# Windowed attention into a SwiGLU block: the opening's value products grouped by row mode, pair 3 on a joined tile, and two gate blocks at once

## The chip, the cores and the metric

The kernel runs on one core of a Trainium2 chip. The metric is the time of one execution on the device in microseconds (us), the median of several runs. A profile is one more execution, taken by the hardware profiler.

## What is computed

```python
def _attn_ref(q, k, v):                     # q, k, v: (8 batches, 8 heads, 576, 64)
    scores = scale * np.matmul(q, k.transpose(0, 1, 3, 2))
    mask = (rel >= 0) & (rel < 64)          # rel = row position - column position
    scores = np.where(mask, scores, -1e9)
    ...                                     # softmax over the columns
    return np.matmul(attn, v)

def _moe_ref(x, w_gate, w_val, w_out):      # x: 4608 tokens x 512, of the attention's output
    g = x @ w_gate                          # 512 x 1536
    silu = g * (1.0 / (1.0 + np.exp(-g)))
    val = x @ w_val
    return silu * val @ w_out               # 1536 x 512
```

Every token looks at itself and the 63 tokens before it, in each of 8 heads; the heads' outputs side by side are a token's 512 inputs to a gated two-layer block.

## The kernel before

The 4608 tokens are worked off in nine tiles of 512: eight hold rows 0 to 511 of a batch, one (`LAST`) the rows 512 to 575 of all eight. For each tile the kernel makes scores, exponentials, sums and value products, then the gate and value products with `wg` and `wv` in twelve blocks of 128 columns (`gate_value`, L432 to L440: four products of 128x512 with `wg` and four with `wv` to a block), then the projection with `wo` (L445). From the second tile on, the attention of a tile lies among the projection of the one before, so that TensorE always has work.

The order is written out by hand; each engine executes its own instructions in the order in which they stand in the program, and waits only where an operand or a buffer is not ready. Eight PSUM banks are used under the names `bank[0]` to `bank[7]`: banks 0 to 3 are the halves of two double tiles, `two0` and `two1`, banks 4 to 7 are `one0` to `one3`. In the profile all of them show as `two` and `one`.

The change touches the opening, tile 0, for which nothing can be prepared. Its heads are handled as four pairs `u` = 0 to 3. `scores_first(u)` (L233) writes a pair's scores into `two0` or `two1`, `weigh_first(u)` (L563) takes their exponential on ScalarE (ACT) into `eb[u]`, `sums_first(u, b)` (L568) sums them over the rows with a product with ones (L295) and gives two functions that make the inverse of the sums on ACT, a logarithm (L316) and an exponential (L319).

`part_first(us, x, ms)` (L345) issues the value products of tile 0. A pair's output has eight blocks `m` of 64 tokens. An odd block needs the 64 keys of its own block and the 64 before it, which lie in the same tile of 128 value rows `v1[:, m // 2]`: one product over 128 rows for each head `h`. An even block's keys lie in two neighbouring tiles, in rows 64 to 127 of the one before (`x` = 1) and in rows 0 to 63 of its own (`x` = 0): two products over 64 rows each, block 0 only one. A pair thus has 22 products. Pairs 0 to 3 accumulate in banks `aos = (4, 5, 0, 1)`.

Products over the upper and the lower 64 rows of the array may run at the same time, and both kinds add to the same bank. `marker` (L358) is a small product over all rows that stands between them; `look` (L361) issues a marker and lets VectorE (DVE) copy one column of it into `seen`.

The four tiles of values come by different ways: `v1[:, 0]` is cast by ACT (L624), `v1[:, 1]` by DVE (L630), both from float32 that SyncE's queue loaded; tiles 2 and 3 come straight into place by two transfers that GpSimd (POOL) issues at 6.6 and 7.7 us. Behind these two, POOL issues the weights in chunks, `wg` and `wv` in turn: for blocks 0 and 1 in two halves each, then 256 columns (two blocks) to a chunk, with a part of the next tile's keys `k_r` and queries `q_s` between them, then `wo` and the next tile's values `vb`.

`scale(t, u, o_ps)` (L382 on) multiplies a pair's output by the inverse sums on DVE and writes a quarter `c` = `u` of `xT` (L392). `gate_part(0, (0, 1), pairs, c)` (L412) issues the products of quarter `c` alone for blocks 0 and 1 with `wg` and `wv` (L416), four products, so that the gate stage can begin before all pairs are scaled. The order from the last scores on, before the change, is:

```python
    part_first((0, 1), 1, (2, 6, 4))
    part_first((2,), 1, (2, 6, 4))
    look(7)
    log2, inv2 = sums_first(2, 6)
    part_first((0, 1), 0, (1, 3, 5))
    marker(7)
    ...
    part_first((3,), 0, (1, 3, 5))
    log3, inv3 = sums_first(3, 7)
    ...
    gate_part(0, (0, 1), pairs, 1)
    part_first((3,), 0, (0, 2, 4, 6, 7))
    for c in (2, 3):
        scale(0, c, bank[aos[c]])
        gate_part(0, (0, 1), pairs, c)
```

Half of pair 3's products so stand between the gate parts 1 and 2. Then the twelve blocks follow: for blocks 0 and 1 only `gate_end` (the activation on ACT, L429, and the multiply on DVE, L430), for the others the whole `gate_value` (L436), one block after the other, in banks that alternate between 5 and 7 and 4 and 6. The `mask` for the later tiles is built on DVE after block 2 (L667 to L674). Transposes of `k_r` (L681) stand after blocks 7 and 10.

Of the kernel before, what the change touches and what calls it, by code (L numbers as in the profile page):

```python
# [8 lines left out]
P = 128  # L9
# [8 lines left out]
def kernel(  # L18
# [10 lines left out]
    nc = tc.nc  # L29
    S, D, H = 576, 64, 8  # L30
# [23 lines left out]
    v1 = v12[:, 0]  # L54
# [59 lines left out]
    def second_halves(t, us, a, copy):  # L114

        src, dst = slice(64 * a, 64 * a + 32), slice(64 * a + 32, 64 * a + 64)
        ap = staged[t][0][:, us].rearrange("r u (e d) -> r (u e) d", d=D)
        copy(ap[dst, :, 0:32], ap[src, :, 32:64])
# [78 lines left out]
    def split_k(dst, tp, copy=nc.vector.tensor_copy):  # L197
        copy(  # L198
            dst.rearrange("p (r e) -> p r e", e=4),
            tp.rearrange("p (e r) -> p r e", e=4),  # L200
        )
# [20 lines left out]
    def bias_first(u):  # L222

        for c in range(2):
            for h in range(2):
                r = slice(64 * h, 64 * h + 64)
                nc.tensor.matmul(
                    two[u % 2][64 * c:64 * c + 64, h], identb[r, r],
                    bias[r, c ^ h].rearrange("r e i c x -> r (e i c x)"),
                    start=True, stop=False,  # L230
                )

    def scores_first(u):  # L233

        qT = queries[0][:, u, :]
        for j in range(8):
            c = j % 2
            for h in range(2):
                r = slice(64 * h, 64 * h + 64)
                nc.tensor.matmul(  # L240
                    blocks(two[u % 2][64 * c:64 * c + 64, h], 0, j, min(8, j + 2)),
                    kT[0][r, u, 64 * j:64 * j + 64],
                    blocks(qT[r], 0, j, min(8, j + 2)),
                    start=False, stop=j > 5,
                )
# [3 lines left out]
    def half(x):  # L249
        return slice(64 * x, 64 * x + 64)  # L250
# [60 lines left out]
    def turned(ap):  # L311

        return ap.rearrange("r (e x) -> r x e", e=16)
# [28 lines left out]
        for w in range(2):  # L342
            invert(rs[w])

    def part_first(us, x, ms):  # L345

        for m in ms:
            for u in us:
                r = slice(0, P) if m % 2 else half(x)
                for h in range(2):  # L350
                    nc.tensor.matmul(  # L351
                        blocks(bank[aos[u]][half(h)], 0, m, m + 1),
                        v1[r, m // 2 if m % 2 or not x else m // 2 - 1, 2 * u + h, :],
                        blocks(weights[0, u][r, h, :], 0, m, m + 1),
                        start=(m, x) == (2, 1), stop=m == 7,
                    )

    def marker(b):  # L358
        nc.tensor.matmul(bank[b][0:D, 0:16], ones[:, 0:D], ones[:, 0:16])

    def look(b):  # L361
        marker(b)
        nc.vector.tensor_copy(seen[:], bank[b][0:D, 0:1])

    def mix(t, w, o):
        E = [weights.pop((t, w, h))[0] for h in range(2)]
# [18 lines left out]
    def scale(t, u, o_ps):  # L385
        if u == 0:
            xT[t] = att.tile([P, 4, 512], BF16, name="xT", tag="xT")
        x, r = xT[t][:, u, :], inverse.pop((t, u))
        if t == NT - 1:
            x, o_ps = x.rearrange("r (x e) -> r x e", e=16), turned(o_ps)  # L390
            r = r.rearrange("r (x e) -> r x e", e=16)
        nc.vector.tensor_mul(x, o_ps, r)  # L392
# [10 lines left out]
    def d_tile():  # L403
        return bank[6 + take("v")]

    def mix_all(t):
# [3 lines left out]
        for u in range(4):  # L410
            scale(t, u, tiles[u // 2][:, u % 2])

    def gate_part(t, ms, tiles, c):
        for i, w in enumerate((wg, wv)):
            for m, pair in zip(ms, tiles):
                nc.tensor.matmul(  # L416
                    pair[i], w[:, c, P * m:P * m + P], xT[t][:, c, :],
                    start=(c == 0), stop=(c == 3),
                )

    def gate_tiles():
        return out_tile(), d_tile()

    def gate_end(t, m, pair):
        if m == 0:
            hT[t] = hpool.tile([P, 12, 512], BF16, name="hT", tag="hT")
        g_ps, v_ps = pair
        sg = fsb.tile([P, 512], FP32, name="sg", tag="sg")
        nc.scalar.activation(sg[:], g_ps[:], AF.Silu)  # L429
        nc.vector.tensor_mul(hT[t][:, m, :], sg[:], v_ps[:])  # L430

    def gate_value(t, m):  # L432
        pair = gate_tiles()
        for ps, w in zip(pair, (wg, wv)):
            for c in range(4):
                nc.tensor.matmul(  # L436
                    ps[:], w[:, c, P * m:P * m + P], xT[t][:, c, :],
                    start=(c == 0), stop=(c == 3),
                )
        gate_end(t, m, pair)  # L440
# [32 lines left out]
    def out_tile():  # L473
        return bank[4 + take("g")]
# [33 lines left out]
    set_exp()  # L508
    nc.vector.memset(ones[:, 0:P], 1.0)
    nc.vector.memset(ones[:, P:512], 1.0)  # L510
    make_identity(nc, identb[:])
    warm = bank[7]

# [34 lines left out]
    on_v, on_p, on_a = nc.vector.tensor_copy, nc.gpsimd.tensor_copy, nc.scalar.copy  # L548
# [14 lines left out]
    def weigh_first(u):  # L563
        E = eb[u][:, 1:17].rearrange("r (h y) z -> r h (y z)", h=2)
        nc.scalar.activation(E, two[u % 2][:], AF.Exp, scale=0.125)
        weights[0, u] = E

    def sums_first(u, b):  # L568
        totals_first(u, bank[b])
        inverse[0, u] = room(1)[:, 0]  # L570
        return lambda: log(inverse[0, u], bank[b]), lambda: invert(inverse[0, u])
# [51 lines left out]
    log1()  # L623
    on_a(v1[:, 0], v_first[:, 0])  # L624
    weigh_first(2)
    bias_first(3)
    scores_first(3)
    weigh_first(3)
    inv1()
    on_v(v1[:, 1], v_first[:, 1])  # L630
    aos = (4, 5, 0, 1)
    part_first((0, 1), 1, (2, 6, 4))
    part_first((2,), 1, (2, 6, 4))
    look(7)
    log2, inv2 = sums_first(2, 6)
    part_first((0, 1), 0, (1, 3, 5))
    marker(7)
    part_first((0, 1), 0, (0, 2, 4, 6, 7))
    part_first((2,), 0, (1, 3, 5, 0, 2, 4, 6, 7))
    log2()  # L640
    inv2()
    part_first((3,), 1, (2, 6, 4))
    pairs = [(bank[4], bank[6]), (bank[2], bank[3])]
    scale(0, 0, bank[aos[0]])
    look(3)
    part_first((3,), 0, (1, 3, 5))
    log3, inv3 = sums_first(3, 7)
    log3()
    inv3()
    gate_part(0, (0, 1), pairs, 0)  # L650
    scale(0, 1, bank[aos[1]])
    gate_part(0, (0, 1), pairs, 1)
    part_first((3,), 0, (0, 2, 4, 6, 7))
    for c in (2, 3):
        scale(0, c, bank[aos[c]])
        gate_part(0, (0, 1), pairs, c)
    taken["g"] = taken["v"] = 1
    set_silu()
    for m in range(12):
        if m < 2:  # L660
            gate_end(0, m, pairs[m])
        else:
            gate_value(0, m)
        if m == 2:
            for x in range(2):
                for c in range(2):
                    nc.vector.tensor_copy(  # L667
                        mask[half(x), 0, c],
                        tri[half(x), x ^ c].rearrange("r (y e) -> r e y", e=16),
                    )  # L670
            for i in (1, 2, 4):
                nc.vector.tensor_copy(mask[:, i:2 * i], mask[:, 0:i])
            for E in eb:
                nc.vector.memset(E[:, 0], 0.0)  # L674
        if m in (7, 10):
            for i in range(2):
                u = m // 10 * 2 + i
                tp = two[i].bitcast(BF16)[:, 0, 0:512]
                for e in range(4):
                    for h in range(2):  # L680
                        nc.tensor.transpose(  # L681
                            tp[half(h), P * e:P * e + P], raw_k[:, 2 * u + h, e], identb[:]
                        )
                split_k(kT[1][:, u, :], tp, on_a if u == 2 else on_v)
        if m == 8:
            second_halves(1, lo, 1, on_v)
            second_halves(1, lo, 0, on_a)
        if m == 9:
            for u in range(2):
                turn_q(1, u)  # L690
# [98 lines left out]
```

## Time and profile before

| what | us |
|---|---|
| median of 3 runs | 326.29 |
| the runs | 326.08 to 326.31 |
| profiled execution, its own time | 325.92 |
| its span, first to last instruction | 324.2 |
| PE busy | 315.3 (97%) |
| DVE busy | 218.2 (67%) |
| ACT busy | 166.9 (51%) |
| POOL busy | 145.4 (45%) |

The profile names the engines PE (TensorE; its weight loads are PEld), DVE (VectorE), ACT (ScalarE), POOL (GpSimd) and SP (SyncE). A row of the timeline has the start in us, the length in us, the engine, the line, the operation, what it writes and reads, the shapes and how many instructions were merged; in brackets stands how long the engine had been idle and what ended that. Matmuls overlap in the array, so a single one's length is more than the distance to the next. A row of the chain of waits has the start, the length and the work, merged, with a count. The chain follows what released what, back from the end.

### The profile page before, as it was taken

How to read it: one execution, taken by the hardware profiler on the slowest of the kernel's cores; microseconds unless marked ns; L12 is line 12 of the kernel's file. 1: busy time of each engine (PE TensorE's matmuls, PEld its weight loads, DVE VectorE, ACT ScalarE, POOL GpSimd, SP SyncE). 2: the span in 40 equal slices, each digit the busy share in tenths (PEclk: the TensorE clock that was granted, in tenths of full speed). 3: DMA queues.
4: the chain of work that ended last, by engine and by line, in shares of the span. 5: the costliest groups of instructions: out<-in, count | busy, mean ns of one | idle time of the engine just before them, and what ended most of it. 6: DMA issues, size and time to landing. Idle time of an engine off the chain costs nothing.

```text
span 324.2 us, 7017 instructions
## 1 busy us (share of the span) xinstructions
PE 315.3 (97%) x2738; PEld 151.0 (47%) x2781; DVE 218.2 (67%) x347; ACT 166.9 (51%) x239; POOL 145.4 (45%) x259
## 2 busy tenths in 40 slices
PE   7989999999999999999999999999999999999996
PEld 3644445444544444444444444454444544444443
DVE  4665756498676776887678766876687586774422
ACT  5943666347633673358336743565347633773310
POOL 4955666875085794676224989463200000000000
PEclk9999999999999999999999999999999999999999
DMA  7999999999879999949922999699501400021013
GB/s 250 202 196 198 207 148 197 164 166 114 166 153 200 138 172 188 192 56 227 200 33 32 164 180 95 45 202 189 99 3 30 103 2 0 10 86 40 0 27 104
DMA packets 83521, 40.35 MB, mean 124 GB/s; under 512 B 64160, under 2 KB 78752, under 8 KB 83488
## 3 DMA queue, kind: packets, MB, share of 16 engines
q0 software_dynamic: 51488, 22.59, 58.5%
q1 hardware_dynamic: 31456, 16.79, 21.4%
q10 hardware_dynamic: 544, 0.52, 0.5%
q8 instruction: 21, 0.34, 0.5%
q14 instruction: 12, 0.10, 0.1%
HBM read 53.02 MB, written 9.44 MB: 193 GB/s over the span
## 4 chain that ended last, share of the span: by engine, by line
PE 95%; DMA 1%; issue 1%; DVE 1%; ACT 1%; DVEq 0%
PE one L436 56%; PE one L445 28%; PE two L269 3%; PE two L376 2%; PE one L302 1%; DMA q_f<-in_q_dram 1%; PE one L487 1%; PE one L416 1%; PE one L195 0%; PE two L416 0%; PE two L351 0%; DVE kT L198 0%; PE one L351 0%; PE two L240 0%; PE two L681 0%
## 5 line engine op out<-in xcount | busy, mean ns | idle before, releaser
L429 ACT ACTIVATE sg<-one 128x512 f32<-128x512 f32 x107 | 63.9, 597 | 115.0 <-PE one L436 87.2
L430 DVE TENSOR_TENSOR hT<-sg,one 128x512 bf16<-128x512 f32 x107 | 74.1, 693 | 61.7 <-PE one L436 59.5
L436 PE MATMUL one<-xT,wg 128*128 128x512 bf16 x414 | 108.0, 379 | 0.8
L436 PE MATMUL one<-xT,wv 128*128 128x512 bf16 x416 | 107.2, 379 | 0.2
L445 PE MATMUL one<-wo,hT 128*128 128x512 bf16 x396 | 93.5, 380 | 1.5 <-issue 0.3
L126 POOL DMA_DIRECT2D k_s<-in_k_dram x112 | 60.6, 550 | 25.2 <-DMA q_s<-in_q_dram 17.3
L436 PEld LDWEIGHTS <-wv 128*128 128x128 bf16 x424 | 41.5, 98 | 50.0
L436 PEld LDWEIGHTS <-wg 128*128 128x128 bf16 x424 | 41.3, 98 | 49.7
L445 PEld LDWEIGHTS <-hT 128*128 128x128 bf16 x420 | 39.0, 98 | 46.7 <-issue 2.0
L282 ACT ACTIVATE eb<-two 128x960 bf16<-128x960 f32 (+1 forms) x32 | 29.5, 974 | 15.1 <-PE two L269 15.0
L217 DVE STREAM_TRANSPOSE kT<-k_s 128x512 bf16<-128x512 bf16 x28 | 36.0, 1287 | 0.0
L285 DVE TENSOR_TENSOR eb<-eb,mask 128x960 bf16<-128x960 bf16 (+1 forms) x32 | 21.0, 658 | 11.9 <-ACT eb L282 11.9
L392 DVE TENSOR_TENSOR xT<-two,r 128x512 bf16<-128x512 f32 x34 | 21.7, 685 | 7.6 <-PE two L376 4.8
L177 POOL CAST vb<-v_f 128x512 bf16<-128x512 f32 x20 | 11.4, 617 | 34.3 <-PE one L436 11.7
L319 ACT ACTIVATE r<-r 128x512 f32<-128x512 f32 (+1 forms) x34 | 22.2, 655 | 1.0
L207 DVE STREAM_TRANSPOSE qT<-q_s 128x512 bf16<-128x512 bf16 x32 | 22.2, 700 | 0.1
L316 ACT ACTIVATE r<-one 128x512 f32<-128x512 f32 x31 | 18.3, 590 | 4.8 <-PE one L302 4.7
L91 POOL DMA_DIRECT2D q_s<-in_q_dram x24 | 13.0, 556 | 4.7 <-DVE qT L207 4.7
L290 DVE TENSOR_TENSOR both<-eb 128x512 bf16<-128x512 bf16 x32 | 13.6, 425 | 1.1
L152 POOL DMA_DIRECT2D vb<-in_v_dram x16 | 10.9, 687 | 6.0 <-DMA wo<-in_moe_w_out_dram 3.8
L495 ACT ACT_TABLE_LOAD x9 | 11.5, 1283 | 2.0 <-issue 1.9
L98 POOL DMA_DIRECT2D q_s<-in_q_dram x16 | 8.6, 629 | 7.1 <-DVE qT L207 7.1
(123 smaller groups left out, 192.2 us busy)
## 6 DMA issues: line engine op xcount, KB each, us to landing
k_s<-in_k_dram POOLq DMA_DIRECT2D x112, 56.0 KB, 4.8
q_s<-in_q_dram POOLq DMA_DIRECT2D x24, 248.0 KB, 5.6
v_f<-in_v_dram SPq DMA_DIRECT2D x40, 128.0 KB
wg<-in_moe_w_gate_dram POOLq DMA_DIRECT2D x5, 256.0 KB, 8.9
wv<-in_moe_w_val_dram POOLq DMA_DIRECT2D x5, 256.0 KB, 9.0
q_f<-in_q_dram SPq DMA_DIRECT2D x4, 256.0 KB
wo<-in_moe_w_out_dram POOLq DMA_DIRECT2D x2, 512.0 KB, 10.7
vb<-in_v_dram POOLq DMA_DIRECT2D x16, 64.0 KB, 4.1
```

The costliest lines, as they stand in the source:

```text
L126: nc.gpsimd.dma_start(k_s[p0:p0 + 32, g, :, 0:w], k[b, a:H:2, s:s + P].rearrange("u (r e) d -> r u (e d)", e=4) [:, :, 32 * c:32 * c + w],)
L207: nc.vector.transpose(queries[t][:, u, :].rearrange("r (e x) -> r e x", e=16), staged[t][0][:, u].rearrange("r (e d) -> r e d", d=D)[:, :, ...
L217: nc.vector.transpose(dst[:, u, :].rearrange("r (g x e) -> r g e x", g=4, e=4), k_s[:, :, u].rearrange("r g (e d) -> r g e d", d=D)[:, :, ...
L282: nc.scalar.activation(flat, s_ps[h][:].rearrange("r a b -> r (a b)")[:, 0:n], AF.Exp, scale=0.125)
L285: nc.vector.tensor_mul(flat, flat, mask[:].rearrange("r j c e y -> r (j c e y)")[:, 0:n])
L316: nc.scalar.activation(r, d_ps, AF.Ln)
L319: nc.scalar.activation(r, r, AF.Exp, scale=-1.0)
L392: nc.vector.tensor_mul(x, o_ps, r)
L429: nc.scalar.activation(sg[:], g_ps[:], AF.Silu)
L430: nc.vector.tensor_mul(hT[t][:, m, :], sg[:], v_ps[:])
L436: nc.tensor.matmul(ps[:], w[:, c, P * m:P * m + P], xT[t][:, c, :], start=(c == 0), stop=(c == 3),)
L445: nc.tensor.matmul(o_ps[:], hT[t][:, c, P * s:P * s + P], wo[:, c, :], start=(c == 0), stop=(c == 11),)
```

## The change

The value products of tile 0 are put in another order, with products of one row mode together. Those of pair 3 use a second copy of its values: in `joined`, which lies in the memory of `mask` until that is built, an even block's keys stand in one tile of 128 rows (the last 64 rows of the tile before in the upper half, with zeros there for block 0, and the first 64 rows of its own tile in the lower half), so that each even block is one product over 128 rows. DVE fills `joined` with two copies and a memset. All value products, pair 3's too, stand ahead of the gate parts, and four of pairs 0 and 1 ahead of the last scores. The marker is now a product over the 64 rows whose products stand beside it. After the gate parts, blocks 2 and 3 are issued together: all products with `wg` of both, then all with `wv` of both. The mask is built after block 3 instead of block 2.

```diff
-    def part_first(us, x, ms):
+    def part_first(us, x, ms, last=None):
...
-                        start=(m, x) == (2, 1), stop=m == 7,
+                        start=(m, x) == (2, 1), stop=m == last,
...
+    joined = mask[:].rearrange("r j c e y -> r (j c e y)")[:, 0:512]
+    joined = joined.rearrange("r (i h d) -> r i h d", i=4, h=2)
+
+    def joined_first(u):
+
+        for m in range(8):
+            for h in range(2):
+                src = v1[:, m // 2, 2 * u + h] if m % 2 else joined[:, m // 2, h]
+                nc.tensor.matmul(
+                    blocks(bank[aos[u]][half(h)], 0, m, m + 1),
+                    src, blocks(weights[0, u][:, h, :], 0, m, m + 1),
+                    start=m == 0, stop=m == 7,
+                )
+
+    def marker(b, x):
+        nc.tensor.matmul(bank[b][0:D, 0:16], ones[half(x), 0:D], ones[half(x), 0:16])
...
+    nc.vector.memset(joined[half(1), 0], 0.0)
...
+    aos = (4, 5, 0, 1)
     bias_first(3)
+    part_first((0, 1), 1, (2,))
     scores_first(3)
     weigh_first(3)
     inv1()
     on_v(v1[:, 1], v_first[:, 1])
-    aos = (4, 5, 0, 1)
-    part_first((0, 1), 1, (2, 6, 4))
+    on_v(joined[half(1), 1:4], v1[half(1), 0:3, 6:8])
+    part_first((0, 1), 0, (1, 5))
+    part_first((0, 1), 1, (6, 4))
     part_first((2,), 1, (2, 6, 4))
-    look(7)
+    marker(7, 1)
+    on_v(seen[:], bank[7][0:D, 0:1])
+    on_v(joined[half(0)], v1[half(0), :, 6:8])
+    part_first((0, 1), 0, (3,))
     log2, inv2 = sums_first(2, 6)
-    part_first((0, 1), 0, (1, 3, 5))
-    marker(7)
-    part_first((0, 1), 0, (0, 2, 4, 6, 7))
-    part_first((2,), 0, (1, 3, 5, 0, 2, 4, 6, 7))
+    part_first((0, 1), 0, (7,))
+    marker(7, 0)
+    for u in range(3):
+        part_first((u,), 0, (0, 2, 4, 6), 6 if u < 2 else None)
+    scale(0, 0, bank[aos[0]])
     log2()
     inv2()
-    part_first((3,), 1, (2, 6, 4))
-    pairs = [(bank[4], bank[6]), (bank[2], bank[3])]
-    scale(0, 0, bank[aos[0]])
-    look(3)
-    part_first((3,), 0, (1, 3, 5))
     log3, inv3 = sums_first(3, 7)
     log3()
     inv3()
-    gate_part(0, (0, 1), pairs, 0)
-    scale(0, 1, bank[aos[1]])
-    gate_part(0, (0, 1), pairs, 1)
-    part_first((3,), 0, (0, 2, 4, 6, 7))
-    for c in (2, 3):
-        scale(0, c, bank[aos[c]])
+    part_first((2,), 0, (1, 3, 5, 7), 7)
+    joined_first(3)
+    pairs = [(bank[4], bank[6]), (bank[2], bank[3])]
+    for c in range(4):
+        if c:
+            scale(0, c, bank[aos[c]])
         gate_part(0, (0, 1), pairs, c)
     taken["g"] = taken["v"] = 1
     set_silu()
     for m in range(12):
-        if m < 2:
+        if m < 4:
+            if m == 2:
+                pairs += [gate_tiles(), gate_tiles()]
+                for i, w in enumerate((wg, wv)):
+                    for n in (2, 3):
+                        for c in range(4):
+                            gate_one(0, n, pairs[n][i], w, c)
             gate_end(0, m, pairs[m])
         else:
             gate_value(0, m)
-        if m == 2:
+        if m == 3:
```

`gate_one` is the single product that `gate_part` issued before.

More of the change, by code (lines that the diff above doesn't have):

```diff
@@ L354, in part_first @@
                         blocks(weights[0, u][r, h, :], 0, m, m + 1),
-                        start=(m, x) == (2, 1), stop=m == 7,
+                        start=(m, x) == (2, 1), stop=m == last,
                     )
[L358 to L363, printed above, removed]
+    joined = mask[:].rearrange("r j c e y -> r (j c e y)")[:, 0:512]
[11 more added lines that the diff above has]
+        nc.tensor.matmul(bank[b][0:D, 0:16], ones[half(x), 0:D], ones[half(x), 0:16])
     def mix(t, w, o):
@@ L411, in mix_all, with gate_one @@
             scale(t, u, tiles[u // 2][:, u % 2])
+    def gate_one(t, m, ps, w, c):
+        nc.tensor.matmul(
+            ps, w[:, c, P * m:P * m + P], xT[t][:, c, :], start=(c == 0), stop=(c == 3)
+        )
     def gate_part(t, ms, tiles, c):
@@ L415, in gate_part @@
             for m, pair in zip(ms, tiles):
[L416 to L419, printed above, removed]
+                gate_one(t, m, pair[i], w, c)
     def gate_tiles():
```

## The prediction

> **What bounds the kernel now.** I read the page first, for the engine that fills the span, then the chain of waits of the first 60 us, then the timeline of the opening, and last the landing of single transfers.
>
> ```profile
> span 324.2 us, 7017 instructions
> PE 315.3 (97%) x2738; PEld 151.0 (47%) x2781; DVE 218.2 (67%) x347; ACT 166.9 (51%) x239; POOL 145.4 (45%) x259
> PE 95%; DMA 1%; issue 1%; DVE 1%; ACT 1%; DVEq 0%
> ```
>
> TensorE (PE) is the chain for 95% of the span. Once the gate products run without a hole, whatever moves their start moves the end by as much, as long as nothing that does not move with PE (a transfer) is late. So the question is: when does the first whole gate step (L436) begin, and does the rest follow?
>
> The chain of waits around the change (start, length, engine and line, count):
>
> ```profile
> 11.90 0.39 PE two L240 x14
> 12.29 0.18 PE one L351 x8
> 12.95 0.24 PE one L295 x2
> 13.19 0.19 PE one L351 x12
> 13.38 0.55 PE one L351 x20
> 13.94 0.70 PE two L351 x22
> 14.87 0.22 PE one L295 x2
> 15.09 0.32 PE one L416
> 16.93 0.41 PE two L351 x10
> 17.43 0.70 DVE xT L392
> 18.17 0.38 PE one L416
> 20.06 5.83 PE one L436 x27
> 36.27 0.57 PE two L681 x16
> 48.84 0.97 PE two L376 x64
> ```
>
> The value products (L351) of head pairs 0 to 3 run from 12.29; gate parts (L416) start; then ten value products of pair 3 at 16.93, and PE stands until DVE (VectorE) has scaled pair 2. The timeline of the same stretch shows the hole:
>
> ```profile
> 11.77 0.66 DVE L630 CAST v<-v_f 128x512 bf16<-128x512 f32 x1
> 13.81 0.59 ACT L316 ACTIVATE r<-one 128x512 f32<-128x512 f32 x1
> 14.02 0.69 DVE L392 TENSOR_TENSOR xT<-one,r 128x512 bf16<-128x512 f32 x1 [0.88 <-PE one L351]
> 14.43 0.63 ACT L319 ACTIVATE r<-r 128x512 f32<-128x512 f32 x1
> 15.02 0.39 PE L416 MATMUL one<-xT,wg 128*128 128x512 bf16 x1
> 17.43 1.29 DVE L392 TENSOR_TENSOR xT<-two,r 128x512 bf16<-128x512 f32 x2 [1.83 <-PE two L351]
> 18.17 0.38 PE L416 MATMUL one<-xT,wg 128*128 128x512 bf16 x1 [0.86 <-DVE xT L392]
> 19.90 1.03 PE L436 MATMUL one<-xT,wg 128*128 128x512 bf16 x4
> ```
>
> DVE itself was idle for 1.83 us before scaling pair 2. It waited for PE: pairs 2 and 3 share the buffer `two0`, and the wait that the scale gets ends with pair 3's last products, which stand behind half of the gate parts. The first whole gate step begins at 19.90.
>
> **Unit prices.** The chain's x12, x20 and x22 rows hold products of one size. Twelve in one row mode take 0.19, so 0.0158 each. The x20 row changes mode twice (64 rows, 128 rows): 0.55 - 20 x 0.0158 leaves 0.23, so 0.117 a change. The x22 row changes three times: 0.70 - 22 x 0.0158 = 0.35, again 0.117. A gate product costs 5.83 / 27 = 0.216; the 16 of the gate parts cost 3.45 with no hole. Before, they took 19.90 - 15.02 = 4.88, so 1.43 went into the hole and the ten products.
>
> **Part 1: products regrouped, pair 3 joined.** Before, from the end of the last scores (12.29) to the first gate product, PE does 78 value products (12 + 6, 12, 20, 22, 6), seven mode changes, three markers and two pairs of totals. After, pair 3 takes 16 full-row products instead of 22; four products of pairs 0 and 1 go ahead of the last scores; and all of pair 3 comes before the gates: 88 - 6 - 4 = 78 again. But there are five mode changes (to 128 rows for blocks 1 and 5, to 64, to 128 for blocks 3, 7 and the totals, to 64 for the even blocks, to 128 for the rest) and two markers.
> Sum: 78 x 0.0158 = 1.23, 5 x 0.117 = 0.59, totals 0.24 + 0.22, markers 0.03: 2.30. The chain's stretch was 15.09 - 12.29 = 2.80, so gates start 0.50 earlier, at 14.52. The difference is two changes (0.23), a marker, and the old wait of about 0.2 for the second value tile's cast (DVE, ends 12.43), which the blocks 1 and 5 now fill.
> The four early products need the first value tile's cast on ACT and lie in PE's old wait for the last key split (before 11.90): nothing, or, if the cast were late, that lateness on all that follows.
>
> **Part 2: new DVE work.** A zero fill of 64x128 lies in DVE's idle start: nothing. Two copies into the joined tile, 64x384 and 64x512, stand in DVE's queue behind the cast that ends at 12.43, and ahead of the first scale. Their nearest row, that of the POOL transfer that ran beside it, and the transfers of the last two value tiles, for the fourth of which the second copy waits:
>
> ```profile
> 23.46 0.88 DVE L672 COPY mask<-mask 128x128 bf16<-128x128 bf16 x3
> 23.51 0.75 POOL L181 DMA_DIRECT2D wv<-in_moe_w_val_dram  x1 [0.42 <-DMA wg<-in_moe_w_gate_dram]
> L144 POOL DMA_DIRECT2D v<-in_v_dram x2: 891/969/1047, 6.6 to 7.7; - x2
> DMA to landing us min/median/max: 5.2/5.4/5.5
> ```
>
> Those three copies (128, 256 and 512 columns) take 0.88 together, so the new ones, 896 columns as well, should take at most about that, and from below nothing. I take the upper end. The fourth tile lands at 7.7 + 5.2 = 12.9, before the second copy's turn. From 12.43, with the small `seen` copy and its marker between them, DVE is free by about 13.5. Pair 0's even blocks leave PE at 12.29 + 1.3 = 13.6 at the latest; the first scale starts then and ends near 14.3, ahead of 14.52. So the copies cost nothing on PE's path; without that cover they would cost up to 0.88.
>
> **Part 3: gate parts in one run.** Scale by scale: pair 0 ends by 14.3, pair 1 by 15.0 (needed at 15.4), pair 2 after its inverse (ACT, ends 15.06) at 15.8 (needed at 16.25). Pair 3's logarithm and inverse follow on ACT at 0.59 and 0.63, so about 16.3; scaled by 17.0, needed at 14.52 + 12 x 0.216 = 17.1. That is close: 0.1 of slack. No hole, so the whole step starts at 14.52 + 3.45 = 17.97 in place of 19.90: a gain of 1.93.
>
> **Part 4: two blocks at once, mask later.** Sixteen products either way: 0. The order (both gate, then both value) asks for the second chunk of `wv` four products (0.86) later. Block 3's gate products now come right behind block 2's, into block 0's bank, which block 0's activation must have left; it can start once the last gate part's first product is done, eight products (1.7) earlier, and takes about as long as the logarithm above, 0.59: nothing. The mask's build on DVE moves behind one more multiply. Before, block 3's multiply stood behind it and the 27 products from 20.06 ran without a hole; now block 4's does, in the same change of banks: nothing.
>
> **What is late next: transfers.** POOL (GpSimd) issues the weights in the same order as before. Each answer below is for one transfer alone (issue time, then us to landing):
>
> ```profile
> L181 POOL DMA_DIRECT2D wv<-in_moe_w_val_dram x1: 735/735/735, 10.7 to 10.7; - x1
> DMA to landing us min/median/max: 5.8/5.8/5.8
> L181 POOL DMA_DIRECT2D wg<-in_moe_w_gate_dram x1: 789/789/789, 11.4 to 11.4; - x1
> DMA to landing us min/median/max: 6.4/6.4/6.4
> L181 POOL DMA_DIRECT2D wv<-in_moe_w_val_dram x1: 806/806/806, 13.6 to 13.6; - x1
> DMA to landing us min/median/max: 8.4/8.4/8.4
> L77 POOL DMA_DIRECT2D k_r<-in_k_dram x1: 742/742/742, 24.8 to 24.8; - x1
> DMA to landing us min/median/max: 9.0/9.0/9.0
> L152 POOL DMA_DIRECT2D vb<-in_v_dram x1: 679/679/679, 43.2 to 43.2; - x1
> DMA to landing us min/median/max: 3.1/3.1/3.1
> ```
>
> Half a chunk of `wv` for gate parts 2 and 3 lands at 16.5, needed at 14.52 + 10 x 0.216 = 16.7. `wg` for blocks 2 and 3 lands at 17.8, needed at 17.97. `wv` for blocks 4 and 5 lands at 22.0, needed 20 products after 17.97, at 22.3. All fit, by 0.2 to 0.3; the last also caps the gain: the whole steps cannot start before 22.0 - 4.32 = 17.7, a gain of 2.2. Further on, the second half of `k_r` lands at 33.8 for transposes (L681) that move from 36.27 to 34.3, and the last of `vb` at 46.3 for products (L376) that move from 48.84 to 46.9. The rest of the chain then moves whole.
>
> **Sum.** 1.93 us off, of the profiled execution's own 325.92 (span 324.2 and 1.7 around it): 324.0. The median of the runs is 326.29, 0.37 above that execution; against it, rounded to 1.9: **324.4**. Lower bound of the gain if the opening saves nothing: 1.43; upper 2.2; so 324.1 to 324.9. Runs scatter by 0.23 (326.08 to 326.31), which widens this to 323.9 to 325.1. A difference of 0.2%, 0.65 us, is about what a measurement tells from none.
>
> **Rivals.**
> *Copies and issues hold each other up.* The two copies run in the time in which POOL issues a transfer every 0.8 us. If a copy had to wait for a running issue to end, the first would end near 13.2 and the second behind the 0.806 us issue of 13.6, at about 14.8; the first scale ends at 15.45, and whole steps start at 18.95: gain 0.95, 325.3. Against it, the three mask copies ran through a POOL issue begun 0.05 after them, in 0.88. For it, the issue there was the later one.
> [...]
> *The weights take the hole's place.* If the chunks land one issue (0.8) later, `wv` for block 4 comes at 22.8 and PE loses 0.5 of the gain: 324.9.
> *The gain is absorbed later*: `k_r` or `vb`, by rows 0.5 early, come 2 us late. 326.3, no change. Nothing on PE waits for a transfer in the chain after 20 us.
> *Slower.* The same weights, delayed for good: POOL sends each transfer once an earlier one is back, so lost issue time could add up. Only if `wv` for block 4 lands over 2.2 us late is the gain used up; at 3.0 late whole steps start at 25.0 - 4.32 = 20.7, 0.8 after the old start: 327.1. Against it: two copies of 0.88 in all cannot hold POOL that long, and transfers land 6 to 8 us after issue, with a queue to live on.
>
> **How the numbers follow.** Forecast 0.72; copies held up 0.08; weights late 0.06; absorbed 0.07; slower 0.07. The first three are faster: 0.86. The range reaches from 323.9 to the held-up copies, 325.3, and leaves out some 0.15.
>
> **What would show it.** Right: no idle PE over 0.2 us between 12.3 and the first whole gate step, which starts near 18.0; transposes of `k_r` near 34.4. Wrong: PE waits for `xT` on DVE (part 2 or 3 mis-sized), for a weight chunk, or the later stages start as late as before.

## The result

The changed kernel took 324.38 us (median of 7 runs, 324.13 to 324.97), the kernel before 326.29 us (7 runs, 325.87 to 327.97): a ratio of 0.9938, 95% interval 0.9919 to 0.9957. The profiled execution took 324.13 us, its span was 322.4.

The page of the changed kernel, with its instruction queue, which is wanted further on:

```profile
span 322.4 us, 7047 instructions
PE 317.1 (98%) x2774; PEld 150.5 (47%) x2774; DVE 219.5 (68%) x349; ACT 166.8 (52%) x239; POOL 145.8 (45%) x259
...
q8 instruction: 21, 0.34, 0.4%
...
PE 95%; DMA 2%; DVE 1%; SPq 1%; issue 0%; DVEq 0%
```

PE is the chain for 95% of the span, as before; the span is 1.8 shorter. Where that comes from is seen when both opening and later stages are cut at the same five events: the last scores, the first gate product, the first whole step, the second transposes of `k_r`, the mixing products with `vb`. A row has the window, its length, then each engine's busy time. The changed kernel first:

```profile
11.72:14.37 2.65, 2.65 (x100) 2.24 (x101) 2.38 (x6) 2.62 (x5) 2.65 (x5) 1.00 1.61 189
14.37:18.09 3.72, 3.62 (x22) 1.57 (x17) 1.82 (x3) 3.36 (x5) 3.06 (x5) 1.00 1.46 195
18.09:34.47 16.38, 16.38 (x91) 7.42 (x91) 11.47 (x26) 7.17 (x12) 8.77 (x14) 1.00 1.39 199
34.47:47.05 12.58, 12.58 (x138) 5.76 (x142) 7.91 (x15) 8.56 (x10) 8.29 (x13) 1.00 1.47 167
```

The kernel before:

```profile
11.90:15.02 3.12, 3.11 (x101) 2.43 (x101) 1.53 (x5) 3.09 (x5) 3.12 (x5) 1.00 1.56 191
15.02:19.90 4.88, 3.97 (x28) 1.88 (x28) 1.87 (x3) 3.00 (x5) 3.60 (x6) 1.00 1.46 199
19.90:36.27 16.37, 16.27 (x89) 7.42 (x91) 11.07 (x26) 7.16 (x12) 8.80 (x14) 1.00 1.36 198
36.27:48.84 12.57, 12.46 (x137) 5.75 (x142) 7.91 (x15) 8.55 (x10) 8.37 (x15) 1.00 1.46 170
```

The first stage shrank from 3.12 to 2.65, the second from 4.88 to 3.72, the third and fourth are as long as before (16.38 for 16.37, 12.58 for 12.57). So the change itself brought 0.47 + 1.16 = 1.63; another 0.18 of the 1.81 by which the whole steps start earlier lies in the last scores, which came at 11.72 instead of 11.90 in this execution. They waited for keys that DVE had still to copy (into `kT`, until 11.67 and 11.85; the scores started 0.05 later in both), not for the few changed products ahead of them, and in variants of the changed kernel that are alike up to there they came at 11.71 to 11.90; the 0.18 is put down to chance. What is won by 18.09 is kept whole.

The timeline of the changed opening:

```profile
11.40 0.25 PE L351 MATMUL one<-eb,v 64*64 64x64 bf16 x4
...
11.61 0.58 DVE L645 CAST v<-v_f 128x512 bf16<-128x512 f32 x1
...
12.28 0.35 DVE L646 COPY mask<-v 64x384 bf16<-64x384 bf16 x1
...
12.65 0.78 POOL L181 DMA_DIRECT2D wg<-in_moe_w_gate_dram  x1
...
12.96 0.58 DVE L652 COPY mask<-v 64x512 bf16<-64x512 bf16 x1
...
13.52 1.29 DVE L402 TENSOR_TENSOR xT<-one,r 128x512 bf16<-128x512 f32 x2
...
14.37 0.39 PE L424 MATMUL one<-xT,wg 128*128 128x512 bf16 x1
...
14.92 0.69 DVE L402 TENSOR_TENSOR xT<-two,r 128x512 bf16<-128x512 f32 x1
...
15.24 0.38 PE L424 MATMUL one<-xT,wg 128*128 128x512 bf16 x1
...
15.72 0.38 PE L424 MATMUL two<-xT,wg 128*128 128x512 bf16 x1
...
16.06 0.69 DVE L402 TENSOR_TENSOR xT<-two,r 128x512 bf16<-128x512 f32 x1 [0.45 <-ACT r L319]
...
17.23 0.38 PE L424 MATMUL one<-xT,wg 128*128 128x512 bf16 x1
...
18.09 1.89 PE L424 MATMUL one<-xT,wg 128*128 128x512 bf16 x8
```

The 0.86 hole is gone: the scale of pair 2 starts at 14.92, pair 3 is scaled by 16.75, and the fourth gate part follows at 17.23 without a wait. One stop that nothing forecast is left: the product of 15.24 should be followed 0.22 later, at 15.46, and the next starts at 15.72. That is 0.26 us, on no wait that the row names, so not every stop of an engine in these traces is a wait for an operand or a buffer that the record shows. That stop is what most of the later runs are about.

### The profile page after: what moved, and what is told of

Same layout as the page of the kernel before. It is cut to its first block, busy times and chain, and to the rows that moved or that the text cites. A ratio compares the mean times of both kernels' runs of the same rounds, so it can differ in the third digit from the quotient of the medians.

```text
span 322.4 us, 7047 instructions
## 1 busy us (share of the span) xinstructions
PE 317.1 (98%) x2774; PEld 150.5 (47%) x2774; DVE 219.5 (68%) x349; ACT 166.8 (52%) x239; POOL 145.8 (45%) x259
## 3 DMA queue, kind: packets, MB, share of 16 engines
q1 hardware_dynamic: 31456, 16.79, 21.0%
## 4 chain that ended last, share of the span: by engine, by line
PE 95%; DMA 2%; DVE 1%; SPq 1%; issue 0%; DVEq 0%
PE one L448 56%; PE one L457 29%; PE two L269 3%; PE two L386 2%; DMA k_f<-in_k_dram 2%; PE one L424 2%; PE one L302 1%; PE one L499 1%; SPq L77 1%; PE two L424 1%; DVE kT L198 0%; PE two L702 0%; PE one L351 0%; DVE qT L573 0%; PE two L302 0%
## 5 line engine op out<-in xcount | busy, mean ns | idle before, releaser
L448 PE MATMUL one<-xT,wg 128*128 128x512 bf16 x416 | 106.8, 379 | 0.0
L457 PE MATMUL one<-wo,hT 128*128 128x512 bf16 x420 | 95.2, 380 | 0.0
L448 PEld LDWEIGHTS <-wv 128*128 128x128 bf16 x416 | 40.7, 98 | 49.1
L448 PEld LDWEIGHTS <-wg 128*128 128x128 bf16 x416 | 40.5, 98 | 48.8
```

What stands on the lines that cost most here:

```text
L448: nc.tensor.matmul(ps[:], w[:, c, P * m:P * m + P], xT[t][:, c, :], start=(c == 0), stop=(c == 3),)
L457: nc.tensor.matmul(o_ps[:], hT[t][:, c, P * s:P * s + P], wo[:, c, :], start=(c == 0), stop=(c == 11),)
```

## The experiments

**What the hole was made of.** The theory: pair 2's scale waits because it shares `two0` with pair 3, whose last ten products stand behind two gate parts. First, in the kernel before, only that scale was moved ahead of the ten products.

```diff
     gate_part(0, (0, 1), pairs, 1)
+    scale(0, 2, bank[aos[2]])
     part_first((3,), 0, (0, 2, 4, 6, 7))
-    for c in (2, 3):
-        scale(0, c, bank[aos[c]])
+    for c in (2, 3):
+        if c == 3:
+            scale(0, c, bank[aos[c]])
```

> The order before the change, with one statement moved: pair 2 is scaled ahead of pair 3's last ten value products instead of behind them. Theory (the hole of 0.86 us is the wait of pair 2's scale for pair 3's products, which share its buffer): the scale runs at about 15.65 instead of 17.43, PE goes from the ten products straight into gate part 2 near 17.3, pair 3's scale follows those products and is ready near 18.1 for gate part 3, and the first whole gate step starts near 19.05: 0.85 less than the order before, some 325.4 us. Rival (the hole is the inverse or the weights coming late, or DVE being busy): the hole stays, 326.3 us.

Measured: 325.39 us (12 runs, 324.98 to 326.66), ratio 0.9970, 0.9955 to 0.9985. Its timeline:

```profile
15.45 0.67 DVE L392 TENSOR_TENSOR xT<-two,r 128x512 bf16<-128x512 f32 x1
...
16.78 0.46 PE L351 MATMUL two<-eb,v 64*64 64x64 bf16 x10
...
17.18 0.39 PE L416 MATMUL one<-xT,wg 128*128 128x512 bf16 x1
...
18.96 0.81 PE L436 MATMUL one<-xT,wg 128*128 128x512 bf16 x3
```

The ten products stay in their place and the gate part follows them at once, at 17.18 for 18.17. So the hole was the wait of a scale on the other half of its tile, and half of the gain could be had by one moved line. Standing behind a product in the program is not enough for such a wait. In the kernel before, pair 1's scale stands behind gate part 0, but shares no tile with it:

```profile
14.93 0.67 DVE L392 TENSOR_TENSOR xT<-one,r 128x512 bf16<-128x512 f32 x1
```

It ran at 14.93, ahead of that part's first product at 15.02.

The reverse in the changed kernel: its joined products put behind gate part 1, so that pair 3 ends late again, with everything else of the change left in.

```diff
-    joined_first(3)
     pairs = [(bank[4], bank[6]), (bank[2], bank[3])]
     for c in range(4):
+        if c == 2:
+            joined_first(3)
```

> The changed kernel with pair 3's sixteen products put behind gate part 1 again; all else stays. Theory: the gates start 0.2 earlier than in the changed kernel, but pair 2's scale waits for pair 3's products again, a hole of 0.6 to 0.9 comes back before gate part 2, and the whole step starts 0.7 to 0.9 later than in the changed kernel: some 325.2 us. Rival (grouping and joined tile make the gain): as fast as the changed kernel, 324.4 us.

Measured: 325.46 us (325.17 to 326.17), ratio 0.9975, 0.9964 to 0.9986; 0.2 to 0.3 above what was expected. The hole is back, of the same length as in the kernel before, and the gates start hardly earlier (2.57 after the last scores, for 2.65), since the first scale ended only at 14.42:

```profile
16.84 1.29 DVE L402 TENSOR_TENSOR xT<-two,r 128x512 bf16<-128x512 f32 x2 [1.82 <-PE two L366]
...
17.59 0.38 PE L424 MATMUL one<-xT,wg 128*128 128x512 bf16 x1 [0.86 <-DVE xT L402]
...
19.31 0.38 PE L424 MATMUL one<-xT,wg 128*128 128x512 bf16 x1
```

**Is the order enough without the regrouping and the joined tile?** In the kernel before, the marker and pair 3's last ten products went ahead of all gate parts:

```diff
+    marker(3)
+    part_first((3,), 0, (0, 2, 4, 6, 7))
     gate_part(0, (0, 1), pairs, 0)
     scale(0, 1, bank[aos[1]])
     gate_part(0, (0, 1), pairs, 1)
-    part_first((3,), 0, (0, 2, 4, 6, 7))
```

> The order before the change, with pair 3's last ten products (and a marker ahead of them) moved ahead of all gate parts; no regrouping, no joined tile, one block at a time. Theory (most of the gain is the run of gate parts without a hole): the ten products, two changes of row mode and the marker's wait put the gate start at about 15.5 instead of 15.0, the 16 gate products then take 3.45, and the whole step starts near 18.95: a gain of 0.95, some 325.35 us. Rival (the gain is the grouping by row mode and the joined tile alone): no gain, 326.3 us. Rival (the hole only moves, since pair 3's inverse then ends last): a new wait of 0.3 or more before gate part 3.

Measured: 326.53 us (median of ten executions from 325.50 to 328.11; two more took 374.01 and 667.48), ratio 1.0006, 0.9985 to 1.0027: as the kernel before, where 325.35 was expected. And in the changed kernel, the joined tile was left out: no copies, no memset, pair 3 in its 22 products with a marker pair between the row modes.

```diff
-    nc.vector.memset(joined[half(1), 0], 0.0)
...
-    on_v(joined[half(1), 1:4], v1[half(1), 0:3, 6:8])
...
-    on_v(joined[half(0)], v1[half(0), :, 6:8])
...
-    joined_first(3)
+    part_first((3,), 1, (2, 6, 4))
+    marker(3, 1)
+    on_v(seen[:], bank[3][0:D, 0:1])
+    marker(3, 0)
+    part_first((3,), 0, (0, 2, 4, 6))
+    part_first((3,), 0, (1, 3, 5, 7), 7)
```

> The changed kernel without the joined tile: pair 3 takes 22 products in two row modes with a marker between them, still ahead of the gate parts; the two copies and the zero fill are gone. Theory: 6 products more (0.1), two more changes of row mode (0.23) and the marker's wait for DVE (0.2 to 0.4): the whole step starts 0.4 to 0.7 later than in the changed kernel, some 324.8 to 325.1 us. Rival (the copies cost DVE's chain more than the joined tile saves): as fast or faster than the changed kernel, 324.4 us or less.

Measured: 326.63 us (12 runs, 325.36 to 330.23), ratio 1.0022, 0.9995 to 1.0048. Both medians missed by over 1 us, and both kernels have executions of several kinds. Five runs of the first took 325.50 to 326.02 and five of the second 325.36 to 325.92; three and five others had a mean granted clock of 0.995 or less (0.988 once) and took 327.69 to 328.11 and 327.68 to 330.23; two of each lie between, at full clock, with a cause that stays open. Even the five quickest are 0.2 to 0.8 above what was expected. So the order alone does not bring the gain: even the five quickest of the first kernel, 325.75 in the middle, are only some 0.5 below the kernel before, and its ten together are no faster. The timeline of the second, in its full-clock execution of 325.36, shows what the joined tile saves:

```profile
14.88 0.15 DVE L665 COPY seen<-two 64x1 f32<-64x1 f32 x1 [0.22 <-PE two L373]
...
15.08 0.17 PE L373 MATMUL two<-ones 64*64 64x16 bf16 x1 [0.30 <-DVE seen L665]
...
15.71 0.11 PEld L351 LDWEIGHTS <-v 128*64 128x64 bf16 x2 [0.21 <-issue]
...
19.33 0.38 PE L424 MATMUL one<-xT,wg 128*128 128x512 bf16 x1
```

The two row modes of pair 3 are parted here by markers with a copy of DVE's into `seen` between them: PE stands for 0.30, then has the longer row of products, and in it a stop on no wait at all (the products 15.41 and 15.71 should lie 0.03 apart). The whole steps start at 19.33, 7.21 after the last scores of 12.12; in the changed kernel they start 6.37 after them. So 0.84 is lost between the two, where 0.4 to 0.7 was expected. The first kernel's profile is of its 374 us execution (granted clock 0.85, span 371.9), so its times are not compared; but the clock itself, in the column after the busy time, is worth showing:

```profile
16.00:17.00 1.00, 0.34 (x3) 0.85 1.45 196
17.00:18.00 1.00, 1.00 (x3) 0.61 1.45 196
18.00:20.00 2.00, 2.00 (x6) 0.50 1.45 197
...
20.73:22.00 1.27, 1.27 (x7) 0.85 1.44 190
```

After a stretch in which PE has 0.34 of recorded work in 1 us (its longest stop was 0.54; a gate product due at 16.79 has its weight load in the record and is itself missing), the clock fell to a half for 3.41 us, from 17.32 to 20.73, though PE was busy all that time. In an execution of 324 us that is a mean clock of 1 - 0.5 x 3.41 / 324 = 0.995 and 1.7 us lost: the clock of the longer group, and most of the 1.9 to 2.4 by which its three runs lie above the middle one of the five, 325.75. That they had this very dip is inferred from their mean clock, not seen. What sets off the fall stays open; a stop of 0.70 in another variant (eight warm-up products, below) left the mean clock at 0.999 or 1 in all six executions.

**The changed kernel once more,** without an edit, beside three variants of it on one chip:

> The changed kernel once more, as the measure for the three beside it: 324.4 us. If the 0.26 us in which PE stood in gate part 1 without a wait of its own (15.46 to 15.72) is a chance of one execution, it is not in this profile; if it belongs to the program, it is there again, at the same product.

Measured: 324.44 us (324.41 to 324.93), ratio 0.9949, 0.9937 to 0.9960. The stop is there again, at the same product, and longer:

```profile
15.22 0.38 PE L424 MATMUL one<-xT,wg 128*128 128x512 bf16 x1
...
16.01 0.38 PE L424 MATMUL two<-xT,wg 128*128 128x512 bf16 x1 [0.41 <-issue]
```

From 15.22 the next was due at 15.44: 0.57 lost.

**The copies.** The second copy into the joined tile was made three times:

```diff
-    on_v(joined[half(0)], v1[half(0), :, 6:8])
+    for _ in range(3):
+        on_v(joined[half(0)], v1[half(0), :, 6:8])
```

> The changed kernel with DVE's second copy into the joined tile made three times in a row. Theory (the copies lie beside PE's products and have little cover left): each extra copy takes 0.35 to 0.6, the first scale starts 0.7 to 1.2 later, PE waits for it before the gate parts, and the whole step starts 0.6 to 0.9 later (the stand of 0.26 is then hidden): 325.0 to 325.3 us. Rival (a copy that meets a POOL issue waits for its end, 0.8): 1.5 or more later, 325.9 us or more. Rival (the copies are free): 324.4 us.

Measured: 324.59 us (324.28 to 325.19), ratio 0.9956, 0.9942 to 0.9969. A cost of 0.15 over the kernel with one copy, where 0.6 or more was expected:

```profile
13.08 1.07 DVE L653 COPY mask<-v 64x512 bf16<-64x512 bf16 x3
...
13.23 0.81 POOL L181 DMA_DIRECT2D wv<-in_moe_w_val_dram  x1
...
14.07 1.26 DVE L402 TENSOR_TENSOR xT<-one,r 128x512 bf16<-128x512 f32 x2
...
14.80 0.38 PE L424 MATMUL one<-xT,wg 128*128 128x512 bf16 x1 [0.15 <-DVE xT L402]
...
18.25 1.46 PE L424 MATMUL one<-xT,wg 128*128 128x512 bf16 x6
```

Three copies take 1.07, so 0.36 each; the scale comes 0.55 later and PE waits 0.15 for it, and the sixteen gate products run in 18.25 - 14.80 = 3.45 with no stop. Most of what the wait costs, the stop gives back. That is a first sign that the stop has an end in time and not a length of its own.

**The stop.** The theory: it sits at a fixed place of PE's instruction stream, where the next piece of the program has not yet come. In the trace's list the place is weight load 226 (counted from 0, with two sequencer entries at the start), and the packets of the instruction queue (21 of them, 0.34 MB by the page) lie at times of their own. Two more of the short warm-up products, at the very start, put that place two gate products earlier in the work:

```diff
-    for _ in range(6):
+    for _ in range(8):
         nc.tensor.matmul(warm[0:D, 0:P], ones[:, 0:D], ones[:, 0:P])
```

> The changed kernel with eight instead of six of those warming products. Theory (instructions): they are needed two gate products earlier, the stand grows by 0.43 to about 0.7, and the time by as much: some 324.8 us, more in executions in which the clock then drops to half for 3.4 us (about 2 us each). Rival (weights): the stand stays 0.26, 324.4 to 324.5 us.

Measured: 325.09 us (324.81 to 325.65), ratio 0.9966, 0.9953 to 0.9978; the profiled execution 324.82. The stop moved to the last product of gate part 0, two earlier, and grew:

```profile
15.06 0.38 PE L424 MATMUL one<-xT,wv 128*128 128x512 bf16 x1
...
15.98 0.38 PE L424 MATMUL two<-xT,wv 128*128 128x512 bf16 x1 [0.55 <-issue]
```

It is 0.92 from start to start instead of 0.22: 0.70 lost. The other way, two fewer:

```diff
-    for _ in range(6):
+    for _ in range(4):
```

> The changed kernel with four instead of six of the small products of 128 columns that warm TensorE up at the start. Theory (PE's 0.26 us stand is its instructions: the stand is at the 227th weight load in three kernels, about 2.3 us after a 16 KB transfer of the instruction queue begins): the point where the next instructions are needed falls two gate products (0.43) later, they are there by then, and the stand goes: 0.2 to 0.3 less than the changed kernel, some 324.15 us. Rival (the stand waits for the half chunk of gate weights for parts 2 and 3, which landed at 15.71): no change, 324.4 us, and the stand stays at the same product.

Measured: 325.32 us (8 runs, 323.97 to 325.90), ratio 0.9964, 0.9948 to 0.9979. No stop, and yet slower, but for two runs of 323.97 and 323.98. The reason stands at the other end of the opening: the first eight transposes, of equal work, took 0.62 in the changed kernel and 1.03 here, and eight more at 7.35 were still as slow.

```profile
4.83 1.03 PE L195 MATMUL one<-identb,qk_b 128*128 128x128 bf16 x8 [0.50 <-ACT qk_b L564]
...
7.35 1.04 PE L195 MATMUL one<-identb,qk_b 128*128 128x128 bf16 x8
```

The full clock came at 10.40 in this execution, at 4.0 to 6.3 in the earlier ones shown above that reached it, and the last scores at 13.34 instead of 11.72. That it came too late in most of the eight runs is inferred from their times. The two quickest are 0.46 below the repeat's median, which is what an early clock without the stop would give; no profile shows one. So two variants kept the columns and took instructions away (768 columns in four or in three products instead of six; the first fill of `ones` on DVE grows with them, and the first product starts at 1.20 and 1.26 instead of 1.13):

```diff
-    nc.vector.memset(ones[:, 0:P], 1.0)
-    nc.vector.memset(ones[:, P:512], 1.0)
+    nc.vector.memset(ones[:, 0:192], 1.0)
+    nc.vector.memset(ones[:, 192:512], 1.0)
...
-    for _ in range(6):
-        nc.tensor.matmul(warm[0:D, 0:P], ones[:, 0:D], ones[:, 0:P])
+    for _ in range(4):
+        nc.tensor.matmul(warm[0:D, 0:192], ones[:, 0:D], ones[:, 0:192])
```

> The changed kernel, its six short warm-up products of 128 columns made four of 192: the same 768 columns before the long ones, two products (and two weight loads) fewer in TensorE's stream. Theory (the stand at 15.5 to 16.0 us belongs to a place in TensorE's instruction stream, its weight load number 226, which cannot be had earlier than some 2.3 us after a packet of the instruction queue): that place now lies two gate products (0.43) further on in the work, so the stand shrinks from 0.26 to 0.57 to 0 to 0.14, and the full clock is granted as early as in the changed kernel; 323.8 to 324.2. Rival (the stand belongs to gate part 1, or to what the other engines do at that moment): it stays where it was in the work, 324.4.

Measured: 324.68 us (324.25 to 324.78), ratio 0.9945, 0.9929 to 0.9961. The stop is where the theory puts it, two products further on, at gate part 1's last:

```profile
15.88 0.38 PE L424 MATMUL two<-xT,wg 128*128 128x512 bf16 x1
...
16.09 0.38 PE L424 MATMUL one<-xT,wv 128*128 128x512 bf16 x1
...
16.52 0.38 PE L424 MATMUL two<-xT,wv 128*128 128x512 bf16 x1
```

It cost 0.21. The gain did not come: the last scores were at 12.15, since the first transposes ran slow here too.

```profile
4.87 1.04 PE L195 MATMUL one<-identb,qk_b 128*128 128x128 bf16 x8 [0.26 <-ACT qk_b L564]
```

Such a slow start needs no change of the warm-up: in the kernel without the joined tile, with the six products as they were, the first eight transposes also took 1.03 and the last scores came at 12.12. With three products of 256 columns (the edit is the same with 3 and 256):

> The same with three short warm-up products of 256 columns, three products fewer in the stream. Theory of the instruction stream: place 226 lies 0.65 further on, no stand at all, and all else as in the changed kernel: 323.8 to 324.1, the fastest of all versions. Rival (stand bound to the work): 324.4. If the clock comes later for the wider first product, 325 or more.

Measured: 324.53 us (324.06 to 324.56), ratio 0.9938, 0.9920 to 0.9955. No stop at that place, which PE reached at 16.75. One product of gate part 0 came 0.10 late, at 15.44, for a weight chunk that landed at 15.40; the last scores were at 12.27, because POOL cast a split of `q` only at 6.60 (at 5.84 in the changed kernel). Neither was expected, and no time was gained.

The same warm-up in the kernel before:

> The kernel before with the same three warm-up products of 256 columns. Theory: the kernel before reaches place 226 at 16.85, later than the instructions come, and shows no stand, so there is nothing to take away: 326.3, no change (within 0.2). Rival (the wider warm-up products are better by themselves, in the clock or in the start of the inputs' work): faster by what the changed kernel gains from them, 0.3 to 0.5: 325.9.

Measured: 326.11 us (12 runs, 325.76 to 326.46) beside 326.17 (17 runs, 325.77 to 327.74), ratio 0.9988, 0.9975 to 1.0000: no change that can be told, as expected. It reaches the place at 17.12 and shows no stop.

All fourteen profiles fit one rule. In the seven that stop there, the stop ends 2.24 to 2.41 us after the start of a packet of the instruction queue: changed kernel 13.41 and 15.72, its repeat 13.67 and 16.01, the eight warm-ups 13.69 and 15.98, the four wide ones 14.24 and 16.52, the two kernels with pair 3 unjoined 14.27 and 16.51, 13.30 and 15.71, and one block at a time (below) 13.66 and 16.01. The seven kernels that come to the place later than that go through without a stop (the kernel before: packet 13.71, place 16.86; pair 3 behind, 13.69 and 16.50; three wide, 13.29 and 16.75); the nearest are two fewer, 14.96 and 17.49, and three copies, 13.32 and 15.87, where the place comes 2.53 and 2.55 after the packet and is free.

That PE waits there for its instructions is an inference from these times; no view names the wait. For it speaks that the queue keeps step with PE: its second packet starts when 239 to 247 weight loads have started, in all fourteen profiles. A rival is the half chunk of `wg` for gate parts 2 and 3: in six of the seven it landed 0.01 to 0.14 before the stop's end. Against it, the stop moves with warm-up products added or taken away; in both kernels with pair 3 unjoined it falls among value products, which read no gate weights; and in one of them, with pair 3 ahead, that chunk had landed at 14.74, 1.77 before the stop's end. In the traces of both kernels each of the 21 packets has 16,384 bytes (0.34 MB together). What starts the first packet, and why it comes when it does, stays open.

**Two blocks at once.** In the changed kernel, blocks 2 and 3 were taken one at a time again:

```diff
-        if m < 4:
-            if m == 2:
+        if m < 2:
+            if m == 99:
```

> The changed kernel, with blocks 2 and 3 taken one after the other again (gate, value, gate, value) in place of both gates and then both values. Prediction's part 4: order alone costs nothing, but the next chunk of the value weights, which landed at 18.8 to 19.1, is then needed four products (0.86) after the whole step's start at 18.1, at 18.95, instead of at 19.8: a wait of 0 to 0.2, so 324.4 to 324.6, no change that can be told. Rival (the pairing of blocks 2 and 3 is a part of the gain of its own, for example by the buffers that block 0 and 1 still hold): 0.4 us or more slower than the changed kernel, 324.8 or more.

Measured: 324.40 us (324.13 to 324.94), ratio 0.9941, 0.9924 to 0.9957: as the changed kernel.

```profile
18.38 1.03 PE L448 MATMUL one<-xT,wg 128*128 128x512 bf16 x4
...
19.24 1.03 PE L448 MATMUL one<-xT,wv 128*128 128x512 bf16 x4
```

The chunk of `wv` for blocks 2 and 3, issued at 11.84, landed at 19.08, 0.16 ahead of its first product. In this execution the stop had cost 0.50; without it the product would have been due at 18.74, 0.34 before the chunk. So the pairing does not bring time as things stand. It holds 0.86 in reserve, which would be needed if the stop went.

## Why the prediction was right

**Part 1** held. Gates were to start 0.50 earlier; from the last scores to the first gate product took 2.65 for 3.12, 0.47 less. The four early products did lie ahead of the last scores (11.40), for nothing. That products over the upper and over the lower 64 rows run side by side is seen in the kernel before at 48.84: the mixing products, which change between the two, take 0.97 for 64, 0.0152 each; most have 128 columns, which at a gate product's 0.216 for 512 would be 0.054, 3.6 times as much, while the opening's products of one row mode (0.0158 for 64 columns, by the same reckoning 0.027) gain a factor of 1.7.

**Part 2** held in its outcome. The copies took 0.35 and 0.58, 0.93 together, against an upper end of 0.88, and DVE was free at 13.54 for the first scale. The prediction said that they were covered, and tripling one showed how much cover there is: two more, of 0.36 each, moved the gates by 0.34 against the last scores (2.99 instead of 2.65).

**Part 3** held in its main point, and the slack that worried it was larger. Pair 3 was scaled at 16.75 and wanted at 17.23, 0.48 to spare (the prediction: 17.0 and 17.1); 0.26 of that slack is the stop, which put off the moment at which it was wanted. The step that failed is the price of "gate parts in one run", 3.45: they took 3.72, because of the 0.26 stop. Only there: the gate products themselves kept their 0.216. So of the signs that were to show it right, the start of the whole step (18.09) and the transposes (34.47) are met, and the one of no idle PE over 0.2 us is missed by this stop, counted from start to start.

**Part 4** held: zero. **Transfers** held: chunks landed at 16.2 and 17.5, 0.6 ahead of their use, and PE worked in all of the 16.38 us from the first whole step to the transposes and in all of the 12.58 after that.

**The sum.** 1.93 was forecast for the change's own effect; the profile shows 1.63. Of the 0.30 between, 0.27 lies in the gate parts (0.26 of it the stop) and 0.03 in part 1. The first whole step came at 18.09, near the 17.97 of the prediction, because the last scores happened to be 0.18 earlier. That the median, 324.38, agrees with 324.4 to 0.02 is luck beyond what the steps earned: the profiled executions differ by 325.92 - 324.13 = 1.79, the medians by 1.91.

**The rivals.** *Copies and issues hold each other up* is refuted in its strong form. The copy of 512 columns that took 0.58 here took 0.47 in the repeat, 0.39, 0.35 and 0.29 in other variants, always beside issues of 0.74 to 0.82; in the run with three copies a whole issue (13.23 to 14.04) lies inside their 1.07 (13.08 to 14.15). That one of the two shuts the other out for its whole length does not fit these rows, if an issue's row is the time for which it would hold a copy up: at worst the copy took 0.29 longer than its shortest. What the copy lost those 0.29 to stays open. *The weights take the hole's place*: not in the changed kernel, but 0.10 of it is seen in the variant with three wide products. *Absorbed later* and *slower* are refuted by the equal lengths of the later stages.

## What to carry to other kernels

When a wait names an engine, ask which part of a shared tile it really waits for: here a scale waited for ten products of another pair in the other half of its buffer, and one moved line was worth 0.9 us. Between data-driven stages, cut both traces at the same events and compare lengths; that parts the gain of an edit (1.63) from a start that was early by chance (0.18). A stop that follows no wait (0.21 to 0.70 us here) and stays at the same place of the instruction stream while the work shifts under it made the author suspect the program's own loading, which no view names; two warm-up products more at the start of the program moved it by two gate products. A gap in a list of products has to be compared with the weight loads before it counts as a stop: with pair 3 ahead, the product due at 16.79 is missing from the record and its weight load is in it.

## What was not expected of the hardware

- In seven of fourteen profiles PE stood at one place of its stream, for 0.21 to 0.70 us, until 2.24 to 2.41 us after a 16,384-byte packet of the instruction queue had started; in the seven that came there later after it, 2.53 us or more, it did not stand.
- A stop of 0.54, in an execution already at a granted clock of 0.85, was followed by a clock of a half for 3.41 us, dearer than the stop; a stop of 0.70 at full clock was followed by none.
- The moment of the first full clock differs between executions that start alike: with the same six short warm-up products and six long ones it came at 4.0 to 6.3, and the first transposes took 0.62 in the changed kernel and 1.03 without the joined tile. It came at 6.0 with four wide products and at 10.4 with two short ones fewer; one execution of each is too few to tell the edit from chance. No variant of the warm-up was faster than the changed kernel by its median.
